# Second layer's first product by Strassen's rule: seven products of half size in place of eight, in groups of 512 tokens

## The chip, the cores and the metric

One Trainium2 chip, of which the kernel uses one core. The metric is the device time of one execution in microseconds (us). The engines of a core work side by side, each through its own list of instructions in order: TensorE (PE; its weight loads are shown as PEld), VectorE (DVE), ScalarE (ACT), GpSimd (POOL), and SyncE (SP), which here issues every DMA. They wait for one another through semaphores. TensorE reads SBUF and writes PSUM, which has eight banks of 128 partitions x 512 fp32.

## The reference

Eight batches of 576 tokens, 4608 in all, 512 wide. An attention through 32 packed rows makes x; a first dense layer of 2048 features follows, whose activation is h - tanh(h); then a second layer with eight experts.

```python
attn_out = _attn_ref(q, k, v, p)                  # two small softmax attentions per head
x = attn_out.transpose(0, 2, 1, 3).reshape(4608, 512)
h = x @ w_in                                      # 512 -> 2048
x = (h - np.tanh(h)) @ w_out                      # 2048 -> 512
logits = x @ w_gate + modality_bias[modality_id]  # 8 experts, softmax, argmax
for e in range(8):                                # second layer
    mask = e_idx == e
    h = np.maximum(x[mask] @ w1[e], 0.0)          # 512 -> 1024
    out[mask] = gate_w[mask, None] * (h @ w2[e])  # 1024 -> 512
```

The kernel computes all tokens with the expert that it reads from the first tokens' routing; code behind a flag redoes the others, and is skipped here.

## The kernel before, in words

Every large product is done in three parts: each fp32 operand is split into a high part, rounded to the matmul's type (ScalarE), and the rest (one VectorE or GpSimd subtraction), and `mm3` (lines 103 to 107) issues high x high, low x high and high x low into one PSUM bank.

The work is a list of slots. A slot of the first layer ("a") is one half batch of 288 tokens (`hb`, 16 of them) and one block of 128 features (`f`, 16 of them): 256 slots. TensorE does `gemm1` (two times three matmuls, 288 columns) for slot n and `gemm2` (twelve matmuls) for slot n - 3 (LAG). Between the two stands a chain that changes engine at each step: ScalarE's square `u` and exponential `qq` (`chain`, lines 857, 858), VectorE's `qq` and `gs` (860, 862), ScalarE's `gh` (871) and VectorE's `gl` (872). The bank of `gemm1` is free for slot n + 2 once `gs` has read it. The attention of the next batches fills the gaps until about slot 228. After a half batch `evac` writes x as high and low parts to SBUF, and SP stores them to DRAM (`x_hi`, `x_lo`).

A slot of the second layer ("b") is 256 tokens (`kk`, 18 of them) and one block of 128 features of 1024 (`f`, 8 of them): 144 slots. `gemm1b` (line 956) does four contraction blocks of three matmuls with 256 columns; `relu` (963) makes the high part on ScalarE and the low part on VectorE straight from PSUM; `gemm2b` (979), three slots later, does two times three matmuls with 512 columns into two of four `acc` banks, so that the two banks of the last 256 tokens can be emptied (`evac_b`, 1002) beside the next ones.

The second layer's weights come while the last half batches of the first layer run: `w1_load`, `w1_split` (lines 917 and 926), `w2_load`, `w2_split` (934, 942). ScalarE makes the high parts and GpSimd the low parts. `xb_load` (949) brings the tokens' two parts from DRAM, three buffers deep.

The loop at the end issues, slot by slot, what the tables `pe_ev`, `pre_ev` and `post_ev` hold. A scheduler then sets the final order on each engine, by priorities and its own estimate of durations, and each engine keeps to that order.

Of the kernel before, what the change touches and what calls it, by code (L numbers as in the profile page):

```python
# [26 lines left out]
def attn_moe_moe_kernel(  # L27
# [24 lines left out]
    TB = 256  # L52
# [19 lines left out]
    ps_at = ctx.enter_context(tc.tile_pool(name="ps_at", bufs=1, space=PSUM))  # L72
# [493 lines left out]
    def logits_pe(hb):  # L566
        ps = AT[0:32, 1, 0:HW]
# [7 lines left out]
    def route_in(hb):  # L575
        ps = AT[0:32, 1, 0:HW]
# [340 lines left out]
    def w1_load(bp, f):  # L917
        st = bp.tile([128, 4, 128], F32, name="w1s", tag="ws", bufs=2)
        e = ev_reg["e"]
        nc.sync.dma_start(  # L920
            out=st,
            in_=w1[bass.ds(e, 1)].rearrange("o (k p) c -> p (o k) c", p=128)[:, :, f * 128:f * 128 + 128],
        )
        w1t[f] = st

    def w1_split(bp, f):
        st = w1t[f]
        hi = bp.tile([128, 4, 128], F32R, name=f"w1h{f}")
# [13 lines left out]
    def w2_split(f):  # L942
# [3 lines left out]
        nc.gpsimd.tensor_tensor(out=lo, in0=st, in1=f32(hi), op=ALU.subtract)  # L946
        w2t[f] = (hi, lo)

    def xb_load(kk):
        xb[kk] = [  # L950
            late["x"].tile([128, 4, TB], F32R, name=f"xb{c}", tag=f"xb{c}", bufs=3) for c in "hl"
        ]
        for d, t in zip(xs, xb[kk]):
            nc.sync.dma_start(out=f32(t), in_=d[:, :, kk * TB:kk * TB + TB])

    def gemm1b(n, kk, f):
        ps = ps_h.tile([128, TB], F32, name="h", tag="h")
        xh, xl = xb[kk]
        for c in range(4):
            mm3(ps, (w1t[f][0][:, c, :], w1t[f][1][:, c, :]), (xh[:, c, :], xl[:, c, :]), c == 0, c == 3)  # L960
        ht[n] = ps

    def relu(n):
        ps = ht.pop(n)
        if n % 2:
            gh, gl = (
                gp.tile([128, TB], F32R, name="bg", tag=tg, bufs=2) for tg in ("u", "qq")
            )
        else:
            gh = g3.tile([128, TB], F32R, name="bh", tag="gh")  # L970
            gl = g3.tile([128, TB], F32R, name="bl", tag="gl")
        nc.scalar.activation(out=gh, in_=ps, func=ACTF.Relu)  # L972
        nc.vector.scalar_tensor_tensor(  # L973
            out=gl, in0=ps, scalar=0.0, in1=f32(gh), op0=ALU.max, op1=ALU.subtract
        )
        gt[n] = (gh, gl)
        yield

    def gemm2b(n, kk, f):
        if f == 0:  # L980
            oa[kk] = [
                pools["acc"].tile([128, 512], F32, name=f"acc{2 * (kk % 2) + t}") for t in range(2)
            ]
# [44 lines left out]
    with ExitStack():  # L1028
# [153 lines left out]
        for n, (ph, i, f, first, kind) in enumerate(slots):  # L1182
            if ph == "a" and kind == "full":
# [100 lines left out]
```

## Time and profile before

| | us |
|---|---|
| median of 3 runs (lowest to highest) | 1256.22 (1255.32 to 1256.65) |
| the profiled execution, own time | 1256.98 |
| its span, first to last instruction | 1255.2 |
| TensorE busy | 1195.3 (95%) |
| TensorE weight loads busy | 1050.2 (84%) |
| VectorE busy | 722.7 (58%) |
| ScalarE busy | 569.6 (45%) |
| GpSimd busy | 77.5 (6%) |
| mean granted TensorE clock | 0.98 |

"Busy" counts the time in which an engine has at least one instruction under way. A matmul's row is longer than the distance to the next matmul, since they are pipelined; its pace is read from starts. VectorE and ScalarE rows overlap a little too. In a row, `out<-in` are tile names without buffer numbers; `<-` with an engine in brackets or behind a bar names what ended the wait. In the second layer `h<-xbh,w1h` is `gemm1b`, `acc<-w2h,bh` is `gemm2b`; in the first, `h<-ah,mh` is `gemm1` and `acc<-gh,wo_hi` is `gemm2`.

### The profile page before, as it was taken

What the parts mean: (1) busy time and instruction counts of PE and PEld (TensorE: products, weight loads), DVE (VectorE), ACT (ScalarE), POOL (GpSimd) and SP (SyncE); (2) the same over time, 40 slices, a digit from 0 to 9 for tenths busy, and PEclk for the clock granted to TensorE, in tenths of its full rate; (3) what the DMA queues carried; (4) which work ended last, traced back from release to release, by engine and by line L of the source; (5) the groups of instructions that cost most, each with busy time, mean ns of one, the idle gap of its engine ahead of it and who ended that gap; (6) DMA issues with size and microseconds to landing.
All of it is one profiled execution on the core that took longest, in us unless ns stands there. A gap on an engine that the chain in (4) does not pass through costs nothing.

```text
span 1255.2 us, 24451 instructions
## 1 busy us (share of the span) xinstructions
PE 1195.3 (95%) x9764; PEld 1050.2 (84%) x9765; DVE 722.7 (58%) x1603; ACT 569.6 (45%) x1320; POOL 77.5 (6%) x69
## 2 busy tenths in 40 slices
PE   5698899999999999999999999999999999999996
PEld 3356678799889889889889899998999999999995
DVE  4866897787887787887787876654121111211111
ACT  3688756556556556556556556641111111111111
POOL 1222100000000000000000002310000000000000
PEclk8699999999999999999999999999999999999998
DMA  8768455454454354354354136221222112221201
GB/s 217 225 197 215 134 141 126 123 144 112 106 144 126 82 144 124 82 143 122 82 143 123 51 111 198 88 64 53 85 67 81 58 65 85 66 79 59 67 18 37
DMA packets 193291, 137.54 MB, mean 110 GB/s; under 512 B 123024, under 2 KB 169104, under 8 KB 193168
## 3 DMA queue, kind: packets, MB, share of 16 engines
q1 hardware_dynamic: 193168, 135.90, 39.2%
q8 instruction: 78, 1.28, 0.4%
q14 instruction: 45, 0.37, 0.1%
HBM read 98.10 MB, written 37.75 MB: 108 GB/s over the span
## 4 chain that ended last, share of the span: by engine, by line
PE 78%; DVE 8%; issue 6%; DMA 2%; ACT 2%; POOL 2%; SPq 0%; POOLq 0%; DVEq 0%; ACTq 0%
PE acc L105 15%; PE acc L107 14%; PE acc L106 14%; PE h L106 10%; PE h L105 10%; PE h L107 9%; PE at L212 3%; DVE s L487 1%; PE at L359 1%; POOL wv L188 1%; DVE x2l L906 1%; DVE qq L860 1%; PE h L844 1%; DVE gl L872 1%; DMA raw<-in_moe_w_in_dram 1%
## 5 line engine op out<-in xcount | busy, mean ns | idle before, releaser
L105 PE MATMUL acc<-gh,wo_hi 128*128 128x288 f32 x960 | 294.6, 307 | 2.7 <-DVE part L903 1.6
L107 PE MATMUL acc<-gl,wo_hi 128*128 128x288 f32 x960 | 282.9, 296 | 3.0 <-DVE gl L872 2.8
L106 PE MATMUL acc<-gh,wo_lo 128*128 128x288 f32 x960 | 283.9, 296 | 0.0
L105 PEld LDWEIGHTS acc<-gh,wo_hi 128*128 128x128 f32 x960 | 180.8, 188 | 36.4 <-ACT u L857 17.5
L860 DVE SCALAR_TENSOR_TENSOR qq<-qq,u 128x288 f32<-128x288 f32 x256 | 131.3, 513 | 116.7 <-ACT qq L858 116.5
L107 PEld LDWEIGHTS acc<-gl,wo_hi 128*128 128x128 f32 x960 | 180.6, 189 | 5.9 <-DVE gl L872 5.0
L106 PEld LDWEIGHTS acc<-gh,wo_lo 128*128 128x128 f32 x960 | 180.9, 188 | 2.4 <-issue 1.7
L871 ACT ACTIVATE gh<-gs 128x288 fp32r<-128x288 f32 x240 | 106.7, 445 | 158.7 <-PE acc L106 143.1
L106 PE MATMUL h<-xbh,w1l 128*128 128x256 f32 x576 | 161.3, 280 | 0.0
L107 PE MATMUL h<-xbl,w1h 128*128 128x256 f32 x576 | 160.8, 279 | 0.0
L105 PE MATMUL h<-xbh,w1h 128*128 128x256 f32 x576 | 160.7, 279 | 0.0
L857 ACT ACTIVATE u<-h 128x288 f32<-128x288 f32 x256 | 105.0, 411 | 109.9 <-PE h L107 90.4
L105 PE MATMUL h<-ah,mh 128*128 128x288 f32 x448 | 133.1, 297 | 2.9 <-DVE gs L862 2.1
L106 PE MATMUL h<-ah,ml 128*128 128x288 f32 x448 | 132.3, 295 | 0.0
L107 PE MATMUL h<-al,mh 128*128 128x288 f32 x448 | 131.8, 294 | 0.0
L872 DVE TENSOR_TENSOR gl<-gs,gh 128x288 fp32r<-128x288 f32 x240 | 113.1, 471 | 31.3 <-ACT gh L871 27.4
L973 DVE SCALAR_TENSOR_TENSOR bl<-h,bh 128x256 fp32r<-128x256 f32 x72 | 30.6, 425 | 165.2 <-ACT bh L972 165.2
L858 ACT ACTIVATE qq<-u 128x288 f32<-128x288 f32 x256 | 113.5, 443 | 7.0
L862 DVE SCALAR_TENSOR_TENSOR gs<-qq,h 128x288 f32<-128x288 f32 x256 | 112.5, 440 | 6.2 <-PE acc L881 1.7
L106 PEld LDWEIGHTS h<-xbh,w1l 128*128 128x128 f32 x576 | 108.1, 188 | 6.2
L105 PEld LDWEIGHTS h<-xbh,w1h 128*128 128x128 f32 x576 | 108.2, 188 | 5.8
L973 DVE SCALAR_TENSOR_TENSOR bg<-h,bg 128x256 fp32r<-128x256 f32 x72 | 30.6, 425 | 139.0 <-ACT bg L972 139.0
(167 smaller groups left out, 1958.4 us busy)
## 6 DMA issues: line engine op xcount, KB each, us to landing
ws<-w_in_v SPq DMA_DIRECT2D x56, 512.0 KB
nat<-in_v_dram SPq DMA_DIRECT2D x16, 576.0 KB
x_hi<-x2h SPq DMA_DIRECT2D x16, 576.0 KB
x_lo<-x2l SPq DMA_DIRECT2D x16, 576.0 KB
xbh<-x_hi SPq DMA_DIRECT2D x18, 512.0 KB
xbl<-x_lo SPq DMA_DIRECT2D x18, 512.0 KB
raw<-in_moe_w_in_dram SPq DMA_DIRECT2D x32, 256.0 KB
raw<-in_moe_w_out_dram SPq DMA_DIRECT2D x16, 512.0 KB
```

The source lines that it names most:

```text
L105: nc.tensor.matmul(out=ps, lhsT=ah, rhs=bh, start=first, stop=False)
L106: nc.tensor.matmul(out=ps, lhsT=al, rhs=bh, start=False, stop=False)
L107: nc.tensor.matmul(out=ps, lhsT=ah, rhs=bl, start=False, stop=last)
L188: nc.gpsimd.tensor_tensor(out=v, in0=lo.bitcast(F32), in1=hi.bitcast(F32), op=ALU.mult)
L212: nc.tensor.matmul(out=out_of(g, hh), lhsT=lhs_of(g, hh), rhs=rhs_of(g, hh), start=True, stop=True, tile_position=(64 * g, 32 * hh),)
L857: nc.scalar.activation(out=u, in_=ps, func=ACTF.Square)
L858: nc.scalar.activation(out=qq, in_=u, func=ACTF.Exp, scale=-PK)
L860: nc.vector.scalar_tensor_tensor(out=qq, in0=qq, scalar=PB, in1=u, op0=ALU.add, op1=ALU.mult)
L862: nc.vector.scalar_tensor_tensor(out=gs, in0=qq, scalar=PA, in1=ps, op0=ALU.mult, op1=ALU.mult)
L871: nc.scalar.activation(out=gh, in_=gs, func=ACTF.Copy)
L872: nc.vector.tensor_tensor(out=gl, in0=gs, in1=f32(gh), op=ALU.subtract)
L973: nc.vector.scalar_tensor_tensor(out=gl, in0=ps, scalar=0.0, in1=f32(gh), op0=ALU.max, op1=ALU.subtract)
```

## The change

The second layer's first product is cut into 2 x 2 blocks: contraction halves (`kh`), feature halves (`fh`) and token halves (`th`) of a group that is now 512 tokens. With A the blocks of w1 and B those of x, Winograd's form of Strassen's rule is used:

- weights: S1 = A21 + A22, S2 = S1 - A11, S3 = A11 - A21, S4 = A12 - S2, made once (`w1_steps`) and split like A11, A12, A22: fourteen pairs of tiles, seven for each of the two contraction blocks of a half;
- tokens: T1 = B12 - B11, T2 = B22 - T1, T3 = B22 - B12, T4 = T2 - B21, made for each group (`x_comb`, eight VectorE sums with 128x512) and split (`x_split`, four times one ScalarE and one VectorE instruction). B11, B21, B22 are used as the two parts that lie in DRAM;
- products: P1 = A11 B11, P2 = A12 B21, P3 = S4 B22, P4 = A22 T4, P5 = S1 T1, P6 = S2 T2, P7 = S3 T3, each six matmuls with 256 columns (`prod`).

A unit `j` (36 of them, four in a group) is one block of 128 features of each half with all 512 tokens of its group: 42 matmuls in `first_b`, then 24 matmuls with 512 columns in `gemm2b` for the unit before, into four `acc` banks of one group. Bank `a` takes P1, then P6, then P7 on top; bank `e` takes P5, then P3; two `h` banks take P2 and P4. ScalarE copies P1, P5 and P1 + P6 out of PSUM in between, and VectorE makes the four blocks of h from banks and copies. `relu_b` then splits the four blocks, now from SBUF. All low parts move from GpSimd to VectorE. In the last half batch of the first layer the feature blocks run 8 to 15 and then 0 to 7. The routing of the last half batch runs beside units 1 and 8.

```diff
@@ constants, pools
-    TB = 256
+    TB = 512
-    ps_at = ctx.enter_context(tc.tile_pool(name="ps_at", bufs=1, space=PSUM))
+    ps_at = tc.alloc_tile_pool(name="ps_at", bufs=1, space=PSUM, side="right")
@@ second layer's weights
-        nc.gpsimd.tensor_tensor(out=lo, in0=st, in1=f32(hi), op=ALU.subtract)
+    def split(tile_of, t):
+        hi, lo = (tile_of(c) for c in "hl")
+        nc.scalar.activation(out=hi, in_=t, func=ACTF.Copy)
+        nc.vector.tensor_tensor(out=lo, in0=t, in1=f32(hi), op=ALU.subtract)
+        return hi, lo
+    def w1_steps(bp, c):
...
+        return [
+            lambda: load("A21", "ah0", 0, 1), lambda: load("A22", "al0", 1, 1), lambda: load("A11", "ah1", 0, 0),
+            lambda: comb("S1", "S", "A21", "A22", ALU.add),
+            lambda: put(5, "S1"), lambda: put(4, "A22"), lambda: load("A12", "al0", 1, 0),
+            lambda: comb("S3", "A21", "A11", "A21", ALU.subtract), lambda: put(7, "S3"),
+            lambda: comb("S2", "S", "S1", "A11", ALU.subtract), lambda: put(6, "S2"), lambda: put(1, "A11"),
+            lambda: comb("S4", "S", "A12", "S2", ALU.subtract), lambda: put(3, "S4"), lambda: put(2, "A12"),
+        ]
@@ tokens
+    def x_load(g):
+        t = [x_tile(F32) for _ in range(4)]
...
+    def x_comb(g):
+        t = xr[g]
+        b11, b21, b22 = ([f32(x) for x in xa[g][p]] for p in (1, 2, 3))
+        for o, a, b, op in (
+            (t[0], t[0], t[1], ALU.add), (t[1], *b11, ALU.add), (t[2], *b22, ALU.add), (t[3], *b21, ALU.add),
+            (t[1], t[0], t[1], ALU.subtract), (t[0], t[2], t[0], ALU.subtract),
+            (t[2], t[2], t[1], ALU.subtract), (t[3], t[2], t[3], ALU.subtract),
+        ):
+            nc.vector.tensor_tensor(out=o, in0=a, in1=b, op=op)
+            yield
@@ one unit
-        for c in range(4):
-            mm3(ps, (w1t[f][0][:, c, :], w1t[f][1][:, c, :]), (xh[:, c, :], xl[:, c, :]), c == 0, c == 3)
+    def first_b(j):
+        a, e = pools["b"].tile([128, 512], F32, name="ba")[:, 0:256], pools["b"].tile([128, 512], F32, name="be")[:, 0:256]
+        d, d2 = h_tile()[:, 0:256], None
+        prod(j, 1, a, True)
+        prod(j, 2, d, True)
+        g_copy(j, "p1", a)
+        nc.vector.tensor_tensor(out=c_tile(j, 0), in0=d, in1=bank[j, "p1"], op=ALU.add)
+        prod(j, 5, e, True)
+        g_copy(j, "p5", e)
+        prod(j, 6, a, False)
+        g_copy(j, "u2", a)
+        prod(j, 3, e, False)
+        nc.vector.tensor_tensor(out=c_tile(j, 1), in0=e, in1=bank[j, "u2"], op=ALU.add)
+        d2 = h_tile()[:, 0:256]
+        prod(j, 4, d2, True)
+        prod(j, 7, a, False)
+        t = c_tile(j, 3)
+        nc.vector.tensor_tensor(out=t, in0=a, in1=bank[j, "p5"], op=ALU.add)
+        nc.vector.tensor_copy(out=bank[j, "p5"], in_=a)
+        t = c_tile(j, 2)
+        nc.vector.tensor_tensor(out=t, in0=bank[j, "p5"], in1=d2, op=ALU.subtract)
@@ second product
-        for t in range(2):
+        for t in range(4):
+            for fh in range(2):
+                st = tuple(x[:, t // 2, (t % 2) * 128:(t % 2) * 128 + 128] for x in parts[fh])
+                mm3(oa[g][t], st, w2t[i + 4 * fh], i == 0 and fh == 0, i == 3 and fh == 1)
@@ where the pieces are issued
+                at_post(b_mem + (15 * c + i) // 2, step)
+            return [lambda: x_load(g), half, half, *(lambda p=p: x_split(g, p) for p in XORDER)]
+        for fn, m in zip(x_steps(0), (-9, -6, -5, -4, -3, -2, -1)):
+            at_post(na + m, fn)
+        for j in range(NU2 + 1):
...
+                    first_b(j)
...
+                threads.append(relu_b(j))
...
+                todo += (xp[0:1], xp[1:2], xp[2:3], xp[3:])[i]
+            if j:
+                gemm2b(j - 1)
+            threads.append(seq(todo))
```

The first place is VectorE near slot 228 of the first layer, where the chain (`qq`, `gs`, `gl`) is all that it does before:

```order
L860 SCALAR_TENSOR_TENSOR qq<-qq,u 128x288
L862 SCALAR_TENSOR_TENSOR gs<-qq,h 128x288
L872 TENSOR_TENSOR gl<-gs,gh 128x288
L860 SCALAR_TENSOR_TENSOR qq<-qq,u 128x288
L872 TENSOR_TENSOR gl<-gs,gh 128x288
L862 SCALAR_TENSOR_TENSOR gs<-qq,h 128x288
```

With the change, the low parts (`wa50l`: product 5, contraction block 0) and the sums of weights (`w1s`) stand between the chain's instructions:

```order
L935 TENSOR_TENSOR wa50l<-w1s,wa50h 128x512
L935 TENSOR_TENSOR wa40l<-w1s,wa40h 128x512
L867 SCALAR_TENSOR_TENSOR qq<-qq,u 128x288
L935 TENSOR_TENSOR wa70l<-w1s,wa70h 128x512
L869 SCALAR_TENSOR_TENSOR gs<-qq,h 128x288
L879 TENSOR_TENSOR gl<-gs,gh 128x288
L867 SCALAR_TENSOR_TENSOR qq<-qq,u 128x288
L956 TENSOR_TENSOR w1s<-w1s 128x512
L869 SCALAR_TENSOR_TENSOR gs<-qq,h 128x288
L879 TENSOR_TENSOR gl<-gs,gh 128x288
```

Twenty such instructions with 128x512 stand in the ten slots 228 to 237, and sixteen (token sums and splits, low parts of w2) in the eight slots 247 to 254.

The second place is ScalarE in the second layer. Before, it does one rectification of a slot after another (`bh`, `bg` from bank `h`):

```order
L972 ACTIVATE bg_12156<-h_12135 128x256
L972 ACTIVATE bh_12179<-h_12160 128x256
L972 ACTIVATE bg_12202<-h_12183 128x256
L972 ACTIVATE bh_12225<-h_12206 128x256
L972 ACTIVATE bg_12248<-h_12229 128x256
```

With the change, in unit 2 (`pc` is a copy of a bank, `ba` and `be` are the banks a and e, `cc` a finished block, `bg` its high part):

```order
L1035 ACTIVATE pc_11546<-ba_11531 128x256
L1070 ACTIVATE bg_11616<-cc_11548 128x256
L1035 ACTIVATE pc_11556<-be_11532 128x256
L1035 ACTIVATE pc_11564<-ba_11531 128x256
L1070 ACTIVATE bg_11616<-cc_11572 128x256
L1070 ACTIVATE bg_11629<-cc_11587 128x256
L1070 ACTIVATE bg_11629<-cc_11590 128x256
```

The rectification of the first block has moved ahead of the copy of bank e (P5). So it stands in 27 of the 36 units; in seven, two token splits with 128x512 stand there.

## Rows read from the trace of the kernel before

**Rows 1.** Busy time by stage: span, each engine (instructions), TensorE clock, DMA share, GB/s

```profile
860.00:900.00 40.00, 40.00 (x259) 35.91 (x258) 8.48 (x23) 6.76 (x16) 0.00 (x0) 1.00 0.18 56
...
1180.00:1220.00 40.00, 40.00 (x258) 36.23 (x257) 7.45 (x16) 6.54 (x16) 0.00 (x0) 1.00 0.09 27
```

**Rows 2.** Groups of instructions from 830 us on: busy, mean ns, idle before

```profile
L106 PE MATMUL h<-xbh,w1l 128*128 128x256 f32 x576 | 161.3, 280 | 0.0
...
L105 PE MATMUL acc<-w2h,bh 128*128 128x512 f32 x144 | 56.9, 395 | 0.0
...
L973 DVE SCALAR_TENSOR_TENSOR bg<-h,bg 128x256 fp32r<-128x256 f32 x72 | 30.6, 425 | 139.0 <-ACT bg L972 139.0
...
L972 ACT ACTIVATE bg<-h 128x256 fp32r<-128x256 f32 x72 | 27.7, 385 | 151.8 <-PE h L107 151.8
```

**Rows 3.** Timeline of one second-layer slot: start, duration in us, engine, line

```profile
940.19 0.28 PE L107 MATMUL h<-xbl,w1h 128*128 128x256 f32 x1
...
940.50 0.38 ACT L972 ACTIVATE bg<-h 128x256 fp32r<-128x256 f32 x1 [2.42 <-PE h L107]
...
940.92 0.42 DVE L973 SCALAR_TENSOR_TENSOR bg<-h,bg 128x256 fp32r<-128x256 f32 x1 [2.38 <-ACT bg L972]
...
941.69 0.28 PE L105 MATMUL h<-xbh,w1h 128*128 128x256 f32 x1
...
943.11 0.39 PE L105 MATMUL acc<-w2h,bg 128*128 128x512 f32 x1
...
944.50 0.28 PE L105 MATMUL h<-xbh,w1h 128*128 128x256 f32 x1
```

**Rows 4.** Who TensorE waited for, 735 to 850 us: total, times, longest

```profile
PE h L105 <- DVE gs L862: 2.1, 3, 1.3
```

**Rows 5.** Groups of VectorE and ScalarE in the steady first layer, 300 to 680 us

```profile
L860 DVE SCALAR_TENSOR_TENSOR qq<-qq,u 128x288 f32<-128x288 f32 x129 | 61.7, 479 | 55.8 <-ACT qq L858 55.8
...
L872 DVE TENSOR_TENSOR gl<-gs,gh 128x288 fp32r<-128x288 f32 x130 | 58.4, 449 | 19.7 <-ACT gh L871 17.6
...
L862 DVE SCALAR_TENSOR_TENSOR gs<-qq,h 128x288 f32<-128x288 f32 x130 | 57.0, 438 | 2.1
...
L244 DVE TENSOR_TENSOR ml<-at,mh 128x512 fp32r<-128x512 f32 x32 | 21.8, 681 | 0.1
...
L858 ACT ACTIVATE qq<-u 128x288 f32<-128x288 f32 x129 | 57.4, 445 | 4.0
...
L857 ACT ACTIVATE u<-h 128x288 f32<-128x288 f32 x129 | 53.1, 412 | 53.6 <-PE h L107 53.6
```

**Rows 6.** Timeline near 765 us, where GpSimd splits weights

```profile
763.27 0.29 PE L106 MATMUL h<-ah,ml 128*128 128x288 f32 x1
...
765.65 0.30 PE L106 MATMUL h<-ah,ml 128*128 128x288 f32 x1
...
765.91 2.75 POOL L931 TENSOR_TENSOR w1l<-w1s,w1h 128x512 fp32r<-128x512 f32 x2 [38.14 <-DMA w1s<-in_moe_w_dram]
...
767.44 1.53 DVE L872 TENSOR_TENSOR gl<-gs,gh 128x288 fp32r<-128x288 f32 x1
```

**Rows 7.** Timeline at 815.5 us: a product releases TensorE

```profile
815.52 0.45 DVE L862 SCALAR_TENSOR_TENSOR gs<-qq,h 128x288 f32<-128x288 f32 x1
...
816.03 0.19 PEld L105 LDWEIGHTS h<-ah,mh 128*128 128x128 f32 x1
...
816.07 0.36 PE L105 MATMUL h<-ah,mh 128*128 128x288 f32 x1
```

**Rows 8.** Timeline near 335 us: three evacuations in a row

```profile
335.49 1.18 DVE L906 TENSOR_TENSOR x2l<-acc,x2h 128x288 fp32r<-128x288 f32 x3
...
334.44 0.99 ACT L905 ACTIVATE x2h<-acc 128x288 fp32r<-128x288 f32 x3
```

**Rows 9.** Chain of waits: start, duration, what; a weight load, and the last piece

```profile
768.69 2.91 DMA w1s<-in_moe_w_dram
...
1243.54 0.75 DVE o L1007
```

More of the change, by code (lines that the diff above doesn't have):

```diff
@@ L685, in redo @@
     def redo():
-        nonlocal evp
+        nonlocal evp, AT
         with ExitStack() as st:
@@ new lines, in attn_moe_moe_kernel, with x_split, prod @@
+    XORDER = (5, 6, 4, 7)
+    def x_split(g, p):
+        hi, lo = xa[g][p]
+        t = xr[g][{5: 1, 6: 2, 4: 3, 7: 0}[p]]
+        nc.scalar.activation(out=hi, in_=t, func=ACTF.Copy)
+        yield
+        nc.vector.tensor_tensor(out=lo, in0=t, in1=f32(hi), op=ALU.subtract)
+        yield
+    bank = {}
+    def prod(j, p, ps, start):
+        g, i = divmod(j, 4)
+        for c in range(2):
+            wh, wl = (t[:, 128 * i:128 * i + 128] for t in wa[p, c])
+            xh, xl = (t[:, c, :] for t in xa[g][p])
+            for m, (a, b) in enumerate(((wh, xh), (wl, xh), (wh, xl))):
+                nc.tensor.matmul(
+                    out=ps, lhsT=a, rhs=b, start=start and c == 0 and m == 0, stop=c == 1 and m == 2,
+                    skip_group_check=True,
+                )
@@ new lines, in relu_b @@
+    def relu_b(j):
+        gt[j] = {}
+        for fh in range(2):
+            tag = 2 * (j % 2) + fh
+            hi, lo = gt[j][fh] = [a2p.tile([128, 2, 256], F32R, name="bg", tag=f"a{c}{tag}") for c in "hl"]
+            for th in range(2):
+                t = bank[j, 2 * fh + th]
+                nc.scalar.activation(out=hi[:, th, :], in_=t, func=ACTF.Relu)
+                yield
+                nc.vector.scalar_tensor_tensor(
+                    out=lo[:, th, :], in0=t, scalar=0.0, in1=f32(hi[:, th, :]), op0=ALU.max, op1=ALU.subtract
+                )
+                yield
@@ L989, in out_rows, with gemm2b @@
+    def gemm2b(j):
+        g, i = divmod(j, 4)
+        if i == 0:
+            oa[g] = [pools["acc"].tile([128, 512], F32, name=f"acc{t}") for t in range(4)]
+        parts = gt.pop(j)
+        for t in range(4):
+            for fh in range(2):
+                st = tuple(x[:, t // 2, (t % 2) * 128:(t % 2) * 128 + 128] for x in parts[fh])
+                mm3(oa[g][t], st, w2t[i + 4 * fh], i == 0 and fh == 0, i == 3 and fh == 1)
     def out_rows(t):
@@ L1038, in attn_moe_moe_kernel @@
         for hb in range(2, NHB):
-            for f in range(NF):
-                slots.append(("a", hb, f, f == 0, "full" if f == NF - 1 else None))
+            fs = list(range(NF)) if hb < NHB - 1 else [*range(NF // 2, NF), *range(NF // 2)]
+            for f in fs:
+                slots.append(("a", hb, f, f == fs[0], "full" if f == fs[-1] else None))
         na = len(slots)
-        for kk in range(NTB):
-            for f in range(NF2):
-                slots.append(("b", kk, f, f == 0, "out" if f == NF2 - 1 else None))
         pe_ev, post_ev = {}, {}
```

206 lines of the change are left out of this document (109 added, 97 removed).

## The prediction

> **What bounds the kernel now.** I read the busy time by stage first. In two 40 us windows of the second layer TensorE is busy for all 40.00 us at clock 1.00, VectorE for about 8 and ScalarE for under 7 [rows 1]. So the second layer is a queue of matmuls with nothing else in sight, and a matmul that goes is worth its full distance to the next one. That distance comes from the timeline, not from the groups, whose 280 and 395 ns overlap [rows 2]: in one slot the twelve `h` matmuls start at 941.69 and the first `acc` matmul at 943.11, the next slot at 944.50 [rows 3]. That is 1.42 / 12 = 0.118 us for 256 columns, 1.39 / 6 = 0.232 us for 512 columns, and 2.81 us for a slot; 144 slots make 404 us. Next I looked at who waits for whom on a product's way out. The last `h` matmul starts at 940.19, ScalarE's reading at 940.50 (0.31 later), VectorE's at 940.92, 0.04 behind ScalarE's end [rows 3]. Back to TensorE I take 0.17 us from VectorE's end to a running matmul: at 815.97 `gs` ends, at 816.03 the weight load starts, and the first matmul is 0.36 long where its followers are 0.29 to 0.30 [rows 6, 7]. Last, the late first layer, where the new weights and token sums are made: its slot is 765.65 - 763.27 = 2.38 us [rows 6], and from 735 to 850 us TensorE waits 2.1 us in all for VectorE's `gs` [rows 4].
>
> **The change, part by part.**
>
> *Products removed.* Before there are 144 x 12 = 1728 `h` matmuls with 256 columns, after 36 units x 42 = 1512. The second product keeps 864 with 512 columns. 216 x 0.1183 = **25.6 us less**. A unit without waits takes 42 x 0.1183 + 24 x 0.232 = 10.5 us, a group 42.
>
> The Trainium skill ("TensorE: Matmul & The Clock Gate", section Back-to-back issue gap) gives about 109 ns between matmuls of 256 columns and 216 ns for 512; by it the 216 matmuls would be worth 23.6 us. The trace shows 118 and 232 [rows 3], some 8% more for both, and it decides.
>
> *Waits inside a unit.* TensorE's order is P1, P2, P5, P6, P3, P4, P7, six matmuls (0.71 us) each. P3 overwrites bank e, so it waits until ScalarE has copied P5; nominally it starts at 24 x 0.1183 = 2.84 us. In ScalarE's order the rectification of block c0 stands ahead of this copy in 27 of 36 units. Its own way is: P2's last matmul starts at 1.30; + 0.31 VectorE makes c0 at 1.61, 0.42 long (the nearest row, a two-input instruction with 256 columns [rows 2]), to 2.03; + 0.04 ScalarE rectifies at 2.07; the copy follows 0.30 to 0.42 later, at 2.37 to 2.49, and takes 0.385 [rows 2], to 2.76 to 2.88; + 0.17 TensorE goes at 2.93 to 3.05. The stall is 0.09 to 0.21 us. The spacing has two ends because instructions in a row start closer than their rows are long: three `x2l` in 1.18 us, 0.39 each, where one of that size alone takes 0.449, and three `x2h` at 0.33 against 0.41 to 0.445 [rows 5, 8]. I take the middle, 0.15 x 27 = 4.1 us. In seven units two token splits with 128x512 stand there, which do not wait for c0: 0 to 0.1 each, 0.7 together. **4.8 us more**; ends 0 and 9. The other waits inside a unit (P6 for the copy of P1, P4 for VectorE's c0 bank, P7 for the copy u2, the second product for the low parts of the unit before) have 0.7 us and more to spare by the same steps; the second product of 24 x 0.232 = 5.6 us stands between a unit and the next and hides the rest: c3, its copy and c2 (3 x 0.42) and the splits.
>
> *VectorE as a whole.* Per unit five instructions on banks and four splits, 9 x 0.42 = 3.8 us; per group 15.1, + 12 sums and splits with 128x512 at 0.60 to 0.68 (`ml` is the row of that shape [rows 5]) = 8.2 at most, + two pieces at 0.75 [rows 9]: 25 of 42 us. ScalarE has seven instructions per unit and stays below 16 of 42. Neither is a bound; what counts is where they stand.
>
> *The late first layer.* VectorE's chain is 0.479 + 0.438 + 0.449 = 1.37 us per slot by rows [rows 5], about 1.2 by spacing. With the change 20 instructions with 128x512 stand in ten slots near 228 to 237, where TensorE needs 10 x 2.38 + 0.6 (about five matmuls at 0.12 for the last attention piece) = 24.4 us. With one `ml` and a reduction still there (1.6, an estimate from the 0.681 of `ml` [rows 5]), VectorE needs 12 + 20 x 0.60 + 1.6 = 25.6 by spacing and 13.7 + 20 x 0.68 + 1.6 = 29 by rows. The chain from one `gemm1` to the use of its bank two slots later has 2 x 2.38 - 0.66 (four of the six matmuls end behind it) - 0.31 - 0.41 - 0.44 - 0.04 - 0.48 - 0.44 - 0.17 = 1.8 us to spare. So VectorE's backlog of 1.2 fits, that of 4.6 does not, and costs 2.8. In slots 247 to 254 sixteen more stand: 19.2 by spacing against 19.0, 21.8 by rows, which overruns by 1.0 at most. Against it stands what leaves: the 2.1 us of TensorE's wait for `gs` [rows 4] fall where GpSimd's 2.75 us splits run, and a `gl` beside them takes 1.53 us where it takes 0.449 elsewhere [rows 5, 6]; that GpSimd work is gone. DMA waits now stand in front of VectorE (a weight load is 2.91 us on the way [rows 9]), but the loads are issued 3 to 4 us ahead: 0 to 1 us. The ends are -2.1, where nothing waits, and +4.8, where rows hold (2.8 + 1.0), a DMA wait of 1 comes and the 2.1 stay. The chain of a slot has been near its limit before, so I take 3 of these 4.8, less the 2.1: **1 us more**.
>
> The Trainium skill ("SBUF — State Buffer", section Who interferes with whom) says that GpSimd and a VectorE instruction with two SBUF inputs lock each other out of a shared port. The 1.53 against 0.449 us [rows 5, 6] agrees. By that rule the 2.1 us vanish in full; by the row alone, one `gl` in a wait, some could stay.
>
> *From the first layer to the second.* Unit 0's first sums stand ahead of the `gl` of the last two slots, whose use has a unit's 5 us to hide in; the routing of the last half batch puts some twenty small VectorE instructions ahead of c0 of unit 2. I take **0.5 us**; ends 0 and 3.3, the latter being a unit's 2.84 us before P3 and one DVE row lost. The four `acc` banks of a group are emptied while the next `first_b` (4.97 us) runs, and two 0.75 us pieces per engine [rows 9] fit; the end of the program is one such piece before and after.
>
> Sum: 1256.98 - 25.6 + 4.8 + 1 + 0.5 = 1236.7 for the profiled execution. The median of the runs is 0.8 lower than that execution, so **1236 us**.
>
> **The rivals.**
>
> *All covers hold* (c0's rectification is short enough, VectorE keeps up): 1256.2 - 25.6 - 2.1 = 1228.5, up to 1231 with a remainder. For it: the spacing of [rows 8], and 0.09 us is little. Against it: the path to P3 is longer than 2.84 even with the short spacing.
>
> *VectorE pays its full rows.* If nothing overlaps between its instructions, the late first layer costs 2.8 + 1.0 - 2.1 + 1 for the DMA waits, about 3, the transition 3.3, and a unit waits 0.21 for P3 and up to 0.3 more where a 128x512 instruction (0.68 [rows 5]) is under way when P2 ends: 27 x 0.5 = 13.5. 1256.2 - 25.6 + 3 + 3.3 + 13.5 = 1250. Against it: VectorE's 0.39 in [rows 8], and its 25 of 42 us.
>
> The Trainium skill ("VectorE: DVE Perf Modes", section The DRAIN you can't avoid) says that the next VectorE instruction cannot start before the pipeline of the last is empty; by it full rows would hold and the time would be near this rival's 1250. Three `x2l` in 1.18 us [rows 8] speak against it here.
>
> *Slower: c0 stands behind long sums in every unit.* If VectorE comes to P2 a whole 128x512 instruction and one split late (0.68 + 0.42 [rows 2, 5]) each time, because the low parts of the last unit run into this one, P3 starts 1.0 us late in all 36 units: 36 us, 1256.2 - 25.6 + 36 = 1267. It decides from 25.6 / 36 = 0.71 us per unit on. For it: c0, the copy and P3 form one chain across three engines in a span of 2 us. Against it: the low parts have the 5.6 us of the second product, and 128x512 instructions are twelve per four units, in units 1 to 3 of a group alone.
>
> **How the numbers follow.** The forecast, 1236 with its own range of 1231 to 1244 (P3 stalls between 1 and 9 us, the late layer between -1 and +4), gets 0.60. The covers hold 0.15; full rows 0.15; the slower rival 0.06; something not seen, to either side, 0.04. What a measurement of this kernel can tell from no change is 0.2%, 2.5 us. Faster by more than that are the first two, the third, and half of the unseen: 0.88 with a little off for an overrun of the third; within 0.2% 0.05, slower 0.07. Range: 1229 to 1250. Below 1229 only a faster pace of the matmuls could go, and above 1250 lie the tail of full rows and the slower rival.
>
> **What would show it.** The groups should have 1512 `h` matmuls at the pace of 0.118, the starts of two units 10.6 to 10.7 us apart, and the list of waits one wait of 0.1 to 0.2 us per unit in front of the first matmul into bank e of P3, ended by ScalarE's copy behind a rectification. From 228 to 254 the waits for `gs` should be a few us, no more. I am wrong if the matmul pace in a unit is not 0.118, if TensorE waits for c0's sum or for the second product's low parts rather than for the copy of P5, or if the late first layer loses more than 5 us.

## The result, and the profile after

| | before | after |
|---|---|---|
| median of the runs, us | 1256.32 (4 runs) | 1235.94 (1235.30 to 1236.33, 4 runs) |
| profiled execution, own time / span, us | 1256.98 / 1255.2 | 1236.33 / 1234.6 |

The ratio of after to before is 0.9839, with a 95% interval of 0.9822 to 0.9856: 1.6% faster. The forecast was 1236. Of its terms the largest came out by itself; the misses of the others nearly cancelled, as the section on the steps shows. The two profiled executions differ by 20.65 us, and that difference is what the following accounts for.

The page's row on busy time, after (engine, busy us, share of the span, instructions):

```profile
PE 1172.3 (95%) x9548; PEld 1028.2 (83%) x9549; DVE 859.2 (70%) x1921; ACT 631.7 (51%) x1470; POOL 56.2 (5%) x53
```

TensorE has 216 instructions fewer than before (9764), and 23.0 us less of busy time. The stage window that answers to the first of [rows 1]:

```profile
860.00:900.00 40.00, 40.00 (x249) 36.06 (x248) 21.61 (x47) 13.49 (x33) 0.00 (x0) 1.00 0.25 79
```

TensorE is still busy throughout at clock 1.00. VectorE is busy for 21.61 us where it was 8.48, ScalarE for 13.49 where it was 6.76: VectorE is at a little over half of the time, ScalarE at a third, and neither is a bound, as in the prediction. These busy 40.00 us hide a wait. One unit in the timeline of after (start, duration, engine, line), from P1's first matmul on:

```profile
906.92 0.29 PE L1028 MATMUL ba<-xw,wa10h 128*128 128x256 f32 x1
...
908.24 0.28 PE L1028 MATMUL h<-xw,wa21h 128*128 128x256 f32 x1
...
908.63 0.42 DVE L1047 TENSOR_TENSOR cc<-h,pc 128x256 f32<-128x256 f32 x1 [4.40 <-PE h L1028]
...
909.09 0.42 ACT L1070 ACTIVATE bg<-cc 128x256 fp32r<-128x256 f32 x1 [0.80 <-DVE cc L1047]
...
909.41 0.36 ACT L1035 ACTIVATE pc<-be 128x256 f32<-128x256 f32 x1
...
909.68 0.29 PE L1028 MATMUL ba<-xw,wa61h 128*128 128x256 f32 x1
909.83 0.39 PE L1028 MATMUL be<-xw,wa30h 128*128 128x256 f32 x1
...
910.05 0.28 PE L1028 MATMUL be<-xw,wa30l 128*128 128x256 f32 x1
```

P2's last matmul (908.24) is followed by c0 on VectorE (908.63), its rectification on ScalarE (909.09), and only then the copy of P5 (909.41 to 909.77). P3's first matmul (`be`, 909.83) starts 0.06 behind the copy's end and is 0.39 long. From P6's last start to P3's second there are 0.37 us, where two steps take 0.24: the wait is 0.13. No row shows it as idle time, since a matmul's row of 0.28 covers it; so the list of waits, in which the prediction expected it, has no such entry. The next unit starts 10.62 us after this one. The starts of all units from 2 on: 29 of 34 show this wait and take 10.62 to 10.69 us (unit 2, beside the routing, 10.81). In 27 of them a rectification stands ahead of the copy, in two (12 and 20) the two token splits. The other five units, 4, 8, 16, 24 and 28, also have token splits there; they take 10.51 to 10.55, but for unit 8, which also holds the flags' two small products.

Who TensorE waited for from 735 us to the end (engine, line, waited for: total, times, longest):

```profile
PE h L105 <- DVE gs L869: 0.7, 1, 0.7
PE ba L1028 <- ACT pc L1035: 0.6, 2, 0.4
PE acc L107 <- DVE gl L879: 0.6, 1, 0.6
```

The first row answers to [rows 4], 0.7 where it was 2.1. VectorE's rows show what this one wait is (1.0 us from start to start): `gs` stands behind a token sum that waited for its load.

```profile
812.40 0.69 DVE L1006 TENSOR_TENSOR xw<-xw 128x512 f32<-128x512 f32 x1 [1.02 <-DMA xw<-x_lo]
```

How long it is differs from execution to execution: up to here the program is the same in after and in experiments 1 to 5 and 10, and their lists have 0.2 to 1.5 us for it. The other two rows lie in the first units. TensorE, ScalarE and VectorE there:

```profile
832.10 0.63 ACT L979 ACTIVATE w2h<-w2s 128x512 fp32r<-128x512 f32 x1 [1.98 <-DMA w2s<-in_moe_w_dram]
...
832.64 0.36 ACT L1035 ACTIVATE pc<-ba 128x256 f32<-128x256 f32 x1
...
833.05 0.39 PE L1028 MATMUL ba<-xw,wa60h 128*128 128x256 f32 x1 [0.43 <-ACT pc L1035]
...
834.47 0.42 DVE L1047 TENSOR_TENSOR cc<-h,pc 128x256 f32<-128x256 f32 x1
...
835.67 0.39 PE L1028 MATMUL ba<-xw,wa70h 128*128 128x256 f32 x1 [0.21 <-ACT pc L1035]
...
840.04 0.80 PE L107 MATMUL acc<-gl,wo_hi 128*128 128x288 f32 x4 [0.64 <-DVE gl L879]
```

ScalarE waits 1.98 us for the last piece of w2 with the copy of P1 queued behind its split; four token sums of the next group run on VectorE ahead of c0 (834.47), and more of them, later, ahead of the last two `gl`. Counted from start to start (with the first matmul behind each, which is 0.1 slower), the three waits cost 0.68, 0.48 and 0.90 us.

The end. The last output piece on VectorE, after, and the bytes that move behind it (time, busy time of PE, PEld, DVE, ACT, POOL, clock, DMA share, GB/s):

```profile
1221.16 0.75 DVE L1106 TENSOR_SCALAR o<-acc,gate_b 128x512 f32<-128x512 f32 x1 [1.97 <-PE acc L107]
```

```profile
1222.00:1223.00 1.00, 0.00 (x0) 0.00 (x0) 0.00 (x0) 0.00 (x0) 0.00 (x0) 1.00 0.27 98
...
1228.00:1229.00 1.00, 0.00 (x0) 0.00 (x0) 0.00 (x0) 0.00 (x0) 0.00 (x0) 0.50 0.26 100
...
1232.00:1233.00 1.00, 0.00 (x0) 0.00 (x0) 0.00 (x0) 0.00 (x0) 0.00 (x0) 0.50 0.05 20
```

And before, whose last piece ends at 1244.29 [rows 9]:

```profile
1249.00:1250.00 1.00, 0.00 (x0) 0.00 (x0) 0.00 (x0) 0.00 (x0) 0.00 (x0) 0.50 0.26 100
...
1252.00:1253.00 1.00, 0.00 (x0) 0.00 (x0) 0.00 (x0) 0.00 (x0) 0.00 (x0) 0.50 0.08 31
```

Before, the span ends 10.9 us behind that instruction; after, 1234.6 - 1221.91 = 12.7. Output leaves at 94 to 109 GB/s in both (1248 to 1251 us before, 1222 to 1230 after), but after the change four pieces of 256 KB are made within 4.8 us, where there were two.

### The profile page after: what moved, and what is told of

It reads as the page before. It is cut to its first block, busy times and chain, and to the rows that moved or that the text cites. A ratio compares the mean times of both kernels' runs of the same rounds, so it can differ in the third digit from the quotient of the medians.

```text
span 1234.6 us, 24553 instructions
## 1 busy us (share of the span) xinstructions
PE 1172.3 (95%) x9548; PEld 1028.2 (83%) x9549; DVE 859.2 (70%) x1921; ACT 631.7 (51%) x1470; POOL 56.2 (5%) x53
## 4 chain that ended last, share of the span: by engine, by line
PE 78%; DVE 10%; issue 5%; DMA 3%; ACT 2%; POOL 1%; SPq 0%; POOLq 0%; DVEq 0%; ACTq 0%
PE acc L105 15%; PE acc L107 14%; PE acc L106 14%; PE ba L1028 6%; PE be L1028 4%; PE h L105 4%; PE h L107 4%; PE h L106 4%; PE h L1028 4%; PE at L212 3%; PE at L359 1%; DVE s L487 1%; POOL wv L188 1%; DVE qq L867 1%; DVE gl L879 1%
## 5 line engine op out<-in xcount | busy, mean ns | idle before, releaser
L867 DVE SCALAR_TENSOR_TENSOR qq<-qq,u 128x288 f32<-128x288 f32 x256 | 123.7, 483 | 98.5 <-ACT qq L865 98.0
L879 DVE TENSOR_TENSOR gl<-gs,gh 128x288 fp32r<-128x288 f32 x240 | 108.8, 454 | 29.9 <-ACT gh L878 26.3
L1070 ACT ACTIVATE bg<-cc 128x256 fp32r<-128x256 f32 x144 | 60.0, 417 | 115.2 <-DVE cc L1053 33.8
L105 PE MATMUL acc<-w2h,bg 128*128 128x512 f32 x288 | 112.5, 391 | 0.0
L106 PE MATMUL acc<-w2h,bg 128*128 128x512 f32 x288 | 112.4, 390 | 0.0
L107 PE MATMUL acc<-w2l,bg 128*128 128x512 f32 x288 | 112.4, 390 | 0.0
L1072 DVE SCALAR_TENSOR_TENSOR bg<-cc,bg 128x256 fp32r<-128x256 f32 x144 | 60.9, 423 | 41.2 <-ACT bg L1070 40.3
L105 PEld LDWEIGHTS h<-ah,mh 128*128 128x128 f32 x448 | 84.0, 188 | 4.5 <-DVE rt_l L588 1.6
L107 PEld LDWEIGHTS h<-al,mh 128*128 128x128 f32 x448 | 84.1, 188 | 0.5 <-issue 0.4
```

Of the source, the lines that this page charges most:

```text
L105: nc.tensor.matmul(out=ps, lhsT=ah, rhs=bh, start=first, stop=False)
L106: nc.tensor.matmul(out=ps, lhsT=al, rhs=bh, start=False, stop=False)
L107: nc.tensor.matmul(out=ps, lhsT=ah, rhs=bl, start=False, stop=last)
L867: nc.vector.scalar_tensor_tensor(out=qq, in0=qq, scalar=PB, in1=u, op0=ALU.add, op1=ALU.mult)
L879: nc.vector.tensor_tensor(out=gl, in0=gs, in1=f32(gh), op=ALU.subtract)
L1070: nc.scalar.activation(out=hi[:, th, :], in_=t, func=ACTF.Relu)
```

## The experiments

Medians are compared with after's 1235.94; each ratio is to the kernel before.

**1. The copy of P5 ahead of every rectification.** ScalarE's order changes in 27 places. VectorE's changes in one, and TensorE's in seven units (4, 8 and so on to 28), where the first matmul of P4 now stands ahead of P3.

```diff
-        nc.scalar.activation(out=t, in_=ps, func=ACTF.Copy)            # g_copy
+        mark[nm] = nc.scalar.activation(out=t, in_=ps, func=ACTF.Copy).ins
...
-                nc.scalar.activation(out=hi[:, th, :], in_=t, func=ACTF.Relu)
+                with tc.issue_after(mark["p5"]):
+                    nc.scalar.activation(out=hi[:, th, :], in_=t, func=ACTF.Relu)
```

Expected: 

> Only ScalarE's order in a unit changes: every rectification stands behind the copy of P5. Theory (P3 waits for this copy because the rectification of c0 runs ahead of it): the gap of 0.1 to 0.13 us in front of P3's second matmul, in 28 units of the changed kernel, shrinks to 0.03 or less, a unit goes from 10.62 to 10.53 us, and the time from 1235.9 to about 1233. Rival (the gap is TensorE's own, from changing between accumulating banks): 10.62 us per unit and 1236 as before. Rival (VectorE is what a unit waits for): the rectification and the low part of c0 come later, the unit gets longer, 1237 or more.

Measured: 1233.10 us, ratio 0.9825 (0.9812 to 0.9838), 2.8 us less than after. In its timeline the same unit:

```profile
907.56 0.39 ACT L1035 ACTIVATE pc<-be 128x256 f32<-128x256 f32 x1 [0.99 <-PE be L1028]
...
907.84 0.41 ACT L1073 ACTIVATE bg<-cc 128x256 fp32r<-128x256 f32 x1
...
907.96 0.29 PE L1028 MATMUL ba<-xw,wa61h 128*128 128x256 f32 x1
908.09 0.29 PE L1028 MATMUL be<-xw,wa30h 128*128 128x256 f32 x1
...
908.22 0.28 PE L1028 MATMUL be<-xw,wa30l 128*128 128x256 f32 x1
```

The copy stands ahead of the rectification, the 0.37 us from 907.96 are 0.26, and a unit takes 10.53 to 10.56, but for unit 8. From the start of unit 2 to that of unit 35 the trace has 348.7 us where after has 351.2; that 2.5 us carries the reading, for the intervals of the two ratios overlap. The theory holds, both rivals fall: it was the place of one 0.42 us instruction.

**2. The eighth product's matmuls put back.**

```diff
         prod(j, 1, a, True)
+        prod(j, 1, a, True)
```

Expected: 

> Product P1 is computed twice (the second overwrites the first), so that a unit has 48 matmuls with 256 columns as the eight products of the plain rule would, and all else is kept, the wait for the copy of P5 too. Theory (a matmul in the second layer is worth its full distance of 0.1183 us): 216 x 0.1183 = 25.6 us more, 1261.5. By the Trainium skill's 109 ns for 256 columns (TensorE: Matmul & The Clock Gate, Back-to-back issue gap): 23.6 us more, 1259.5. Rival (part of the gain came from elsewhere, from the groups of 512 tokens and the order of work): the difference is the same 25.6, but before and this kernel then differ by more than the waits that the traces show (about 5 us).

Measured: 1265.52 us, ratio 1.0075 (1.0059 to 1.0090), 29.6 more than after; 4 us more than expected. From unit to unit the starts are 11.34 to 11.36 us apart in most units where they were 10.62: 0.72 for six matmuls, 0.120 each, 26 us in all. That settles the price (0.118 was used). The 109 ns of the Trainium skill ("TensorE: Matmul & The Clock Gate", section Back-to-back issue gap), which it gives for a matmul by itself at the full clock, do not hold here. Over all units from 2 to 35 the mean step rose by 0.754, since some units also wait longer for c0. Units 0 and 1 take 3.1 us more, 1.4 of them for the twelve matmuls. From unit 0 on this makes 28.7 us; the profiled executions of after and of this kernel already stand 1.0 apart ahead of it, where nothing is changed. In unit 0 TensorE waited 1.79 us for the copy u2, and then its clock fell:

```profile
838.00:839.00 1.00, 0.46 (x4) 0.46 (x5) 0.97 (x3) 0.51 (x3) 0.00 (x0) 1.00 0.00 0
...
840.00:841.00 1.00, 1.00 (x6) 1.00 (x6) 1.00 (x4) 0.67 (x2) 0.00 (x0) 0.50 0.00 0
...
844.00:845.00 1.00, 1.00 (x10) 1.00 (x9) 0.50 (x1) 0.21 (x1) 0.00 (x0) 1.00 0.00 0
```

**3. The copy of P5 made twice.**

```diff
         g_copy(j, "p5", e)
+        nc.scalar.activation(out=bank[j, "p5"], in_=e, func=ACTF.Copy)
```

Expected: 

> ScalarE copies P5 twice in a row in every unit. Theory (P3 waits for ScalarE's copy): the second copy starts about 0.32 us behind the first, so each of the 28 units that waited 0.1 to 0.13 us waits 0.42 to 0.45, and the eight others wait 0.2 to 0.3: 28 x 0.32 + 8 x 0.25 = 11 us more, 1247. Rival (TensorE's own gap): 1236. Rival (ScalarE's work as such, not its place, costs the time): far less than 11, since ScalarE is idle two thirds of a unit.

Measured: 1240.80 us, ratio 0.9884 (0.9869 to 0.9899): 4.9 more, half of what was expected. One unit of it:

```profile
910.23 0.28 PE L1028 MATMUL h<-xw,wa40h 128*128 128x256 f32 x1
910.24 0.39 ACT L1050 ACTIVATE pc<-be 128x256 f32<-128x256 f32 x1
910.35 0.28 PE L1028 MATMUL h<-xw,wa40l 128*128 128x256 f32 x1
...
910.68 0.39 PE L1028 MATMUL be<-xw,wa30h 128*128 128x256 f32 x1
```

The second copy starts 0.40 behind the first and ends at 910.63; P3 (`be`) starts at 910.68, 0.45 behind its place at 910.23, as the theory has it. But two matmuls of P4 (`h`) now fill 0.24 of that: TensorE's order moved with the edit, and they stand ahead of P3. Of the units from 2 on 27 take 10.79 or 10.80, 0.27 more than without a wait and 0.17 more than in after; the other seven, 4, 8 and so on, show no wait and take 10.53, but for unit 8. From the start of unit 2 to that of unit 35 this makes 3.9 us more than in after; 0.8 comes in units 0 and 1. So P3 waits for the copy, and the size was missed because the order moved.

**4. The first units.** The split of w2's last block behind unit 0's copy u2 on ScalarE, and the second group's token sums behind c2 on VectorE.

```diff
+            with tc.issue_after(mark["c2"]) if g == 1 else nullcontext():
                 nc.vector.tensor_tensor(out=o, in0=a, in1=b, op=op)        # x_comb
...
+            with tc.issue_after(mark["u2_0"]) if f == 7 else nullcontext():
+                w2_split(f)
```

Expected: 

> In unit 0, ScalarE's split of the last w2 block is issued behind the copy P1 + P6, and VectorE's token sums of group 1 behind the last block of h; nothing else is changed. Theory (TensorE's three waits between 832 and 840 us, 0.68 + 0.48 + 0.90 us, come from these two placements): 2 us less, 1234. Rival (the waits come from the distance between unit 0's products and the chain of the last slots, whatever stands between): 1236. Rival (the sums moved to units 1 and 2 run into the routing there): 1236 or more, with the waits at P3 of units 1 to 3.

Measured: 1233.68 us, ratio 0.9826 (0.9813 to 0.9840): 2.3 less. TensorE's waits from 735 us to the end shrink to a single row:

```profile
PE h L105 <- DVE gs L869: 0.7, 1, 0.7
```

**5. The last two units tile by tile.** Output tile 2 of both units, then 3, 0 and 1; the last group's banks are emptied in the same order (`evac_b`).

```diff
+    def gemm2b_end(j):
+        for t in (2, 3, 0, 1):
+            for n in (j, j + 1):
+                i = n % 4
+                for fh in range(2):
+                    st = tuple(x[:, t // 2, (t % 2) * 128:(t % 2) * 128 + 128] for x in gt[n][fh])
+                    mm3(oa[j // 4][t], st, w2t[i + 4 * fh], False, i == 3 and fh == 1)
...
-        for t in range(4):
+        for t in (range(4) if g < NTB - 1 else (2, 3, 0, 1)):
```

Expected: 

> The second products of the last two units run tile by tile (output tile 2 of both units, then 3, 0, 1) instead of unit by unit, so that the four output tiles of the last group are finished 2.7 us apart instead of 1.36, and the first one 4 us earlier. Theory (the end of the changed kernel is its four last output pieces of 256 KB going out at about 100 GB/s, 10.5 us from the first piece on, which is why it lasts 12.7 us behind the last VectorE instruction and 10.9 before): the end shortens to about 9.3 us, less 0.2 of a wait for the last low parts: 1236 - 3.3 = 1232.7. Rival (what follows the last VectorE instruction is a fixed cost): 1236.

Measured: 1233.03 us, ratio 0.9811 (0.9796 to 0.9826): 2.9 less. The last VectorE instruction ends at 1221.09 of a span of 1231.5, 10.4 us before its end, not 12.7; bytes leave at 119 GB/s while TensorE still works, and none are left 1.5 us before the end:

```profile
1217.00:1218.00 1.00, 1.00 (x6) 0.84 (x5) 0.00 (x0) 0.38 (x1) 0.00 (x0) 1.00 0.33 119
...
1229.00:1230.00 1.00, 0.00 (x0) 0.00 (x0) 0.00 (x0) 0.00 (x0) 0.00 (x0) 0.50 0.04 14
```

So the end is the output on its way, not a fixed cost. It shortened less than the 3.4 us that were worked out, since the bytes move at only 57 to 90 GB/s behind the last instruction here.

**6 to 9. What the late first layer waited for.** Four kernels: before with the low parts of w1 and w2 on VectorE (6); after with w1's low parts on GpSimd (7); before with four staging buffers for w1, taken from tiles that are free earlier (8); and 8 with the low parts on VectorE (9).

```diff
-        nc.gpsimd.tensor_tensor(out=lo, in0=st, in1=f32(hi), op=ALU.subtract)   # 6 and 9: w1_split, w2_split
+        nc.vector.tensor_tensor(out=lo, in0=st, in1=f32(hi), op=ALU.subtract)
...
-        nc.vector.tensor_tensor(out=lo, in0=t, in1=f32(hi), op=ALU.subtract)    # 7: split
+        nc.gpsimd.tensor_tensor(out=lo, in0=t, in1=f32(hi), op=ALU.subtract)
...
-        st = bp.tile([128, 4, 128], F32, name="w1s", tag="ws", bufs=2)          # 8 and 9: w1_load
+        st = a2p.tile([128, 4, 128], F32, name="w1s", tag=("ah0", "al0", "ah1", "al1")[f % 4])
```

Expected of 6: 

> The kernel before, with the low parts of w1 and w2 made by VectorE instead of GpSimd. Theory (GpSimd's 2.75 us splits hold VectorE's chain up, and cause the waits of 1.49, 0.47 and 0.67 us for gs between 765 and 815 us): these 2.9 us, with the slower start behind each, go; sixteen instructions of 0.6 us fit beside the chain: 1256 - 2.5 = 1253.5. Rival (the chain is so near its limit that whatever is added to VectorE costs as much): 1256 or more.

Expected of 7: 

> The changed kernel, with the fourteen low parts of w1's blocks made by GpSimd again (the sums stay on VectorE). Theory (the same contention): waits for gs near slots 228 to 240 come back, nearly twice as many splits as before: 3 to 5 us more, 1239 to 1241. Rival (VectorE's load in that stretch is what matters, and it loses fourteen instructions of 0.6 us): 1236 or a little less.

Expected of 8: 

> The kernel before with four staging buffers for w1, free earlier, so that ScalarE finds the weights there; the low parts stay on GpSimd. Theory now (two causes of the 2.9 us: ScalarE's split waits 1.55 and 1.59 us for its load in front of u, and GpSimd slows gl or qq beside it): ScalarE's waits for w1s of over a microsecond are gone from the trace; the first four splits stand closer together, so the contention stays or grows: 0 to 2 us less, 1254 to 1256. Rival (GpSimd alone): 1256 or more. Rival (the loads alone): 2.5 us less, 1253.5.

Expected of 9: 

> The same with the low parts on VectorE, as in the changed kernel: both causes are taken away. Theory: the waits of TensorE for gs between 760 and 815 us sum to under 0.7 us, and the time is 1256 less 2 to 2.9, 1253.1 to 1254. Rival (VectorE's sixteen more instructions make up for it): 1256.

| | median, us | ratio to before (95%) |
|---|---|---|
| 6 | 1256.42 | 0.9998 (0.9989 to 1.0007) |
| 7 | 1243.93 | 0.9908 (0.9889 to 0.9927) |
| 8 | 1254.94 | 0.9989 (0.9980 to 0.9998) |
| 9 | 1254.32 | 0.9984 (0.9975 to 0.9993) |

TensorE's waits for `gs` from 735 to 850 us, of 6, 7, 8 and 9 in this order:

```profile
PE h L105 <- DVE gs L862: 1.5, 2, 1.0
```

```profile
PE h L105 <- DVE gs L869: 6.5, 5, 2.6
```

```profile
PE h L105 <- DVE gs L862: 0.5, 2, 0.3
```

```profile
PE h L105 <- DVE gs L862: 0.3, 1, 0.3
```

Experiment 6 speaks against the prediction's reading of [rows 4] as GpSimd's work alone: without GpSimd 1.5 of the 2.1 us stay, and the time is the same. The kernel before shows both of its causes ahead of TensorE's three waits, which end at 769.40, 774.74 and 811.19 us; the third row is from experiment 6.

```profile
765.20 0.63 ACT L930 ACTIVATE w1h<-w1s 128x512 fp32r<-128x512 f32 x1 [1.55 <-DMA w1s<-in_moe_w_dram]
...
809.04 1.36 DVE L860 SCALAR_TENSOR_TENSOR qq<-qq,u 128x288 f32<-128x288 f32 x1 [2.09 <-ACT qq L858]
```

```profile
807.43 0.63 ACT L930 ACTIVATE w1h<-w1s 128x512 fp32r<-128x512 f32 x1 [2.05 <-DMA w1s<-in_moe_w_dram]
```

All three waits do stand beside GpSimd's splits, behind one VectorE row that is too long: the `gl` of [rows 6], a `qq` of 1.33 and this one of 1.36, where 0.46 is usual. But ScalarE is late there too. The weights' split, queued ahead of `u`, waits 1.55, 0.39 and 0.59 us for its load, and the chain with it. In experiment 6 the VectorE rows are 0.45 again, but the waits for loads at these places are 1.56, 1.37 and 2.05, and TensorE still waits.

Loads into other buffers (8) leave 0.5 us of TensorE's waits and are worth 0.1%, barely clear of nothing; both changes together (9) leave 0.3 and are worth 0.16%, 2.0 us, of the 2 to 2.9 expected. That also speaks against the rival of 6, that sixteen more instructions on VectorE cost as much as the waits. But 8 did not do what was expected of its loads: ScalarE's waits of over a microsecond are not gone (1.27, 1.77 and 1.20 in 8, 2.31 and 1.79 in 9); they stand at other places of the chain. So taking GpSimd out alone gains nothing, moving the loads alone a little, and how the 2.1 us divide between the two causes is not shown.

GpSimd does harm where it has enough to do: in 7, fourteen splits beside VectorE's sums cost 8.0 us, more than the 3 to 5 expected, while with the same splits on VectorE, 8.4 us of its time at 0.60 each, TensorE has one wait of 0.7 us. About 1.3 of the 8.0 is TensorE's clock, which fell behind the first long wait (an estimate: twelve matmuls there start 0.24 apart, not 0.13). The sums of 7, beside GpSimd:

```profile
759.92 1.77 DVE L956 TENSOR_TENSOR w1s<-w1s 128x512 f32<-128x512 f32 x1
```

One such sum takes 1.77 us where its kind takes 0.68 without GpSimd (rows at 836.68 us below). The Trainium skill ("SBUF — State Buffer", section Who interferes with whom) has a VectorE instruction with two SBUF inputs and a GpSimd one exclude each other at a shared port; the 1.77 against 0.68 us agree.

**10. All three repairs.** P5 ahead of P2 in TensorE's order, and the edits of 4 and 5.

```diff
         prod(j, 1, a, True)
+        prod(j, 5, e, True)
         prod(j, 2, d, True)
         g_copy(j, "p1", a)
+        g_copy(j, "p5", e)
         nc.vector.tensor_tensor(out=c_tile(j, 0), in0=d, in1=bank[j, "p1"], op=ALU.add)
-        prod(j, 5, e, True)
-        g_copy(j, "p5", e)
```

Expected: 

> Three edits together: P5 is computed ahead of P2 (so that its copy has 0.8 us to spare before P3 and needs no place in ScalarE's order), the placements of e4_first_units, and the last tiles of e5_last_tiles. Theory (the three causes stand apart and add up): 1236 - 2.8 - 2.3 - 3.3 = 1227.5. Rival (TensorE then waits for the next thing, c0 or the copy u2, at the same place): 1231 or more.

Measured: 1227.99 us (1226.14 to 1228.71), ratio 0.9767 (0.9752 to 0.9783): 2.3% less than the kernel before and 7.95 us less than after. The three gains alone (2.8, 2.3 and 2.9) sum to 8.0. Each is known to about 1.6 us by its interval, so they add up as far as that shows, and the closeness is chance. The rival, a next wait at the same place, falls: a unit takes 10.53, but for unit 8, and P3 follows P6 without a gap:

```profile
907.26 0.28 PE L1029 MATMUL ba<-xw,wa61h 128*128 128x256 f32 x1
907.38 0.28 PE L1029 MATMUL be<-xw,wa30h 128*128 128x256 f32 x1
...
907.50 0.28 PE L1029 MATMUL be<-xw,wa30l 128*128 128x256 f32 x1
```

## Why the prediction was right, step by step

| step | predicted, us | in the traces, us |
|---|---|---|
| 216 matmuls | -25.6 | -25.6 to -26 (experiment 2) |
| P3 behind the copy of P5 | +4.8 | +2.9: 29 units by about 0.10 (experiment 1: 2.8) |
| late first layer | +1 | -1.9: waits of 2.9 became 1.0, start to start, in one execution each |
| first units | +0.5 | +2.1 (experiment 4: 2.3) |
| the end | 0 | +1.8 (experiment 5: 2.9 to be had) |
| sum | -19.3 | -20.7; measured -20.65 |

The prediction added its own terms up wrongly: from 1256.98 they give 1237.7, not 1236.7, and 1236.9 for the median. So 1 us of the near hit is that slip; the terms put the time 1 us too high, and that the forecast and the median agree to 0.1 us is luck. After is already 0.5 us ahead of before at 750 us, where nothing is changed, so 20.2 us are to be explained, and the column agrees to no better than half a microsecond.

*Removed matmuls.* Right, in mechanism and size. A unit without waits was put at 10.5 us, and takes 10.53 (experiment 10).

*The wait for the copy of P5.* Right in place and mechanism; mis-sized. The stall was put at 0.09 to 0.21 us with the middle of 0.15. In starts it is 0.11 to 0.14, and a unit is 0.09 to 0.10 longer for it; the 0.7 us for the token splits did not come as such, for five of those seven units do not wait. The sum over three engines came out closer than its parts. In unit 7 c0 starts 0.39 behind P2's last matmul (0.31 was used), the copy starts 0.32 behind the rectification (the middle was 0.36) and is 0.36 long (0.385), and P3's own place is 2.88 behind the unit's start (2.84). The spacing, near its short end of 0.30, is what bears on the rival of full rows. [rows 8] say it more strongly than the prediction read them: three rows of 0.449 within 1.18 us start 0.37 apart, not 0.39, since the last row counts in full. VectorE's rows in unit 0 show the same:

```profile
836.68 0.68 DVE L1006 TENSOR_TENSOR xw<-xw 128x512 f32<-128x512 f32 x1
837.27 0.68 DVE L1016 TENSOR_TENSOR xw<-xw 128x512 fp32r<-128x512 f32 x1
837.88 0.42 DVE L1058 TENSOR_TENSOR cc<-ba,pc 128x256 f32<-128x256 f32 x1
838.21 0.41 DVE L1072 SCALAR_TENSOR_TENSOR bg<-cc,bg 128x256 fp32r<-128x256 f32 x1
```

128x512 instructions start 0.60 us apart and 128x256 ones 0.33, with rows of 0.68 and 0.42. So the rival of full rows had no ground here. The Trainium skill ("VectorE: DVE Perf Modes", section The DRAIN you can't avoid) would have each wait for the last one's end; these rows speak against that, and agree with its exception for instructions that are not held.

*The late first layer.* Two halves. VectorE's added work, 36 instructions with 128x512, fits by spacing as worked out: one wait is left, and it is the wait for a DMA in front of VectorE that the prediction put at 0 to 1 us. Of 3 us of new waits 1.0 came. That the 2.1 us of [rows 4] go (2.9 from start to start) was right, but the reason given was half of it. The failing step is "the 2.1 us of TensorE's wait for `gs` [rows 4] fall where GpSimd's 2.75 us splits run [...]; that GpSimd work is gone". They do fall there, but with GpSimd alone taken out nothing is gained (6): ScalarE's waits for loads stand ahead of the same three waits. In after both are gone; there ScalarE waits for no load from 750 to 826 us.

*The first units.* Mis-sized. It was said that unit 0's sums stand ahead of the `gl` of the last two slots and are hidden; VectorE's list of instructions held the next group's sums there too, and ScalarE's a split with a load to wait for. 2.1 us came of a term of 0.5, within its ends of 0 and 3.3.

*The end.* A term put at nothing. The failed step is "the end of the program is one such piece before and after". The last instruction is the same, but what follows is the output of a whole group of 512 tokens instead of 256: four pieces at 100 GB/s. This term was not in the sum.

The small terms were put at 6.3 us together and measured 4.9: what was missed (1.6 in the first units, 1.8 at the end) and what was put too high (1.9 at P3, 2.9 in the late layer) nearly cancel. The rival of full covers, 1228.5 to 1231, is about where the edits of 1 and 4, which make its covers hold, would bring the kernel: 1235.9 - 2.8 - 2.3 = 1230.8, an estimate, for the two were not run by themselves. Experiment 10 falls below the prediction's 1229 without a faster pace of the matmuls: the rest of its gain is the end, which that sentence had left out.

## What to carry to other kernels

Where an engine is saturated, a removed instruction is worth its start-to-start distance, and the first thing to look for then is who stands ahead of the one copy that frees its bank: moving one rectification per unit out of the way of one copy was worth as much here as 24 of the 216 removed matmuls (2.8 / 0.118). A wait can also have two causes ahead of it: taking one away may gain nothing until the other goes too. A wait shorter than a matmul's row shows in no list of waits; compare starts. And when a group of work is doubled, look at its last one: what leaves at the end doubles too.

## What the runs showed of the hardware

- TensorE's clock: in experiment 2, after a stretch with waits up to 1.79 us (busy 0.46 of the microsecond from 838), the granted clock is 0.50 from 840 to 843 us, 1.2 instead of 2.4 GHz, while TensorE is busy throughout; matmuls with 288 columns start 0.24 us apart, where they take 0.13. In experiment 7 the same happens behind a wait of 2.11 us that ends at 768.47, as the first two windows show (columns as above). But 2.62 us of waiting in the same execution, up to 777.98, leave the clock at 1.00 (third window), as do 1.32 us in before. So the length of one wait does not decide it here; what does is not shown.

```profile
768.00:769.00 1.00, 0.53 (x4) 0.53 (x5) 0.83 (x2) 0.97 (x4) 0.70 (x1) 1.00 0.35 53
771.00:772.00 1.00, 1.00 (x6) 1.00 (x5) 1.00 (x3) 1.00 (x4) 0.99 (x1) 0.50 0.00 0
779.00:780.00 1.00, 1.00 (x10) 1.00 (x9) 1.00 (x1) 0.00 (x0) 1.00 (x1) 1.00 0.00 0
```

- Output of 128x512 tiles left at 94 to 109 GB/s with the DMA engines busy for 0.26 to 0.30 of the time, in before and after, whether two pieces or four were under way. Why no faster was not tried.
